# A segment-recurrent attention and MLP kernel: left outputs in a PSUM bank of their own, and one left K pass in another kind of segment

## The chip, the cores and the metric

One core of one Trainium2 chip. The metric is the device time of one execution in microseconds; the time before is the median of three runs.

## The reference

The input x (2048 tokens of 1024 columns) is normalised, and three things are added: x itself, an MLP with gelu (1024 to 3584 to 1024), and a recurrent attention with 32 heads of 128 columns. The recurrence is what matters here (biases and the batch of 1 left out):

```python
for s in range(64):                                  # segments of 32 tokens
    h = concat([mem, xn[32 * s:32 * s + 32]])        # 8 memory rows + 32 tokens
    q, k, v = h @ Wq, h @ Wk, h @ Wv                 # 1024 -> 32 heads x 128
    p = softmax(mask(q @ k.T * scale))               # memory rows see all, tokens are causal
    o = (p @ v) @ Wo                                 # 4096 -> 1024
    mem = o[:8]                                      # the next segment needs it
    outs.append(o[8:])
```

Everything is bfloat16 in and out. The 64 segments depend on each other through the 8 memory rows.

## The kernel before

A first part (normalisation and MLP) runs up to about 430 us; it leaves x plus MLP output in a DRAM buffer `R_n`, which `turn_R` lays out again into `res_d` (per segment) and `resL_d` (per group). Then comes the loop over the 64 segments, written out by hand, and nearly all of the change lies there.

**Rows.** [...] A segment has 40 rows. So 32 of them are "main" rows (24 tokens and 8 memory rows, tile `hT`) and the last 8 tokens of a segment are "left" rows. The left rows of four segments make one group of 32 rows (`hL`), which goes through the weights once for four segments. Left rows need no memory of their own segment to be projected, so their passes can be made early or late. `hL` has four slots, one for each segment of the group, renewed one after the other for the next group (`load_left_rows` by DMA into a raw place, `renew_left` by VectorE or GpSimd into `hL`).

**Units and kinds.** The weights of a segment are 64 units of 128 x 2048: K, Q and V in halves u = 0 and 1 with eight units each (`half_pass`), then 16 units of O (`o_product`). One unit against one set of rows is four 512-column matmuls on the four column groups of TensorE. 47 units live in SBUF; 17 are "streamed" into six buffers again in every segment, by DMAs on SyncE's queue (`start_stream`, issued when a streamed unit is done), two of them copied by VectorE out of PSUM banks in which they are kept (L283). The kind of a segment is `i4 = s % 4`. The tables `PLACED`, `SCORES_0`, `SUMS_0`, `VALUES_0`, `SUMS_1`, `VALUES_1` say for each kind in which order the units come and behind which unit the scores, the sums of the softmax and the values are put into TensorE's order. Left passes are made in kind 0 (K0 and K1), kind 1 (V0), kind 2 (Q0 and V1) and kind 3 (Q1, and O for the whole group).

**The order in a segment.** K0, Q0, K1 (in it `scores(0)`), Q1 (in it `sums(0)`), V0, V1 (in it `scores(1)`, `values(0)`, `sums(1)`), O (in it `values(1)`), and the turn. `exps`, `weights` and the transposes between them are on ScalarE and VectorE, in order. `weights(0)` writes its second part, `pdB` (L1032), into slot i4 of `ko[0]` in kinds 0, 1 and 3. `ko[u]` holds, slot by slot, first the left keys, then these weights, then the left rows of the attention's output, which kind 3's O product reads. `ko[0]` is the second half of `d_oL`.

**The turn.** The memory rows of O's result become part of the next segment's `hT`: `put_mem` multiplies by an identity into `mixed` (L343), VectorE copies them (L353). While this goes on TensorE is filled with left products of the next segment: `lead_products` makes up to six units of the pass named in L1235 from resident weights, four of them ahead of `put_mem` and two behind. In kinds 0 to 2 O's main result is made in two halves of a PSUM bank and added up (`fold`, L1233). In kind 3 one bank holds left and main rows side by side, eight 512-column matmuls for a unit, and ScalarE copies it out (L1229).

**Outputs.** VectorE adds the residual (L1252), and the rows go out by DMAs: in kinds 0 to 2 four on `loads` (ScalarE's queue in the first seven segments, then GpSimd's), in kind 3 two on ScalarE's queue and six on GpSimd's.

**PSUM.** Three banks rotate (`new_acc`, `let_go`), one is `mixed`, four keep streamed units. 

Of the kernel before, what the change touches and what calls it, by code (L numbers as in the profile page):

```python
# [14 lines left out]
ALU = mybir.AluOpType  # L15
# [53 lines left out]
LATE_FROM = 5  # L69
BEGUN = 4  # L70
# [56 lines left out]
def kernel(  # L127
# [244 lines left out]
    with tc.tile_pool(name="ma", bufs=2) as ma:  # L372
# [138 lines left out]
        def with_left(seg):  # L511

            return seg % GRP == GRP - 1

        def turn_R(ttg, eng, small=None):

            for i in range(4):
                seg = 4 * ttg + i  # L520
                rows = R_n[seg * SEG:(seg + 1) * SEG, :].rearrange("t (j c) -> t j c", j=4)
                og, slot = divmod(seg, GRP)
                both = [
                    t.rearrange("(h r) c -> r h c", h=2)
                    for t in (res_d[GRP * og + GRP, :, :], resL_d[og, :, :])
                ]
                halves = [rows.rearrange("t (h w) c -> t w h c", w=2)[:, w, :, :] for w in range(2)]
                if with_left(seg):
                    m0 = SEG
                    pairs = [(both[w][m0:m0 + SEG, :, :], halves[w]) for w in range(2)]  # L530
                else:
                    pairs = [(res_d[seg + 1, :, :].rearrange("(j t) c -> t j c", j=4), rows)]
                pairs += [(both[w][slot:SEG:GRP, :, :], halves[w][NX:SEG, :, :]) for w in range(2)]
# [220 lines left out]
    with tc.tile_pool(name="late", bufs=1) as late:  # L754
# [67 lines left out]
        raw_2, raw_3, raw_01 = VL[1][:, 0:64], VL[0][:, 256:320], VL[0][:, 256:384]  # L822
        led = {}

        for s in range(NSEG):
# [12 lines left out]
            left_k = [i4 == 0] * 2  # L838
# [94 lines left out]
            def turn_kL(ps, u):  # L933
                turn(ps, ko[u], nc.vector.tensor_copy if first else nc.scalar.copy)
# [24 lines left out]
            def scores(u):  # L959
# [12 lines left out]
                for j in range(4):  # L972
                    q = slice(32 * j, 32 * j + 32)
                    nc.tensor.matmul(  # L974
                        sB[q, :, :, :], lhsT=keys[:, j, :, i4], rhs=qL_ends[:, 4 * j:4 * j + 4, :, :],
# [63 lines left out]
            def values(u, rs):  # L1039

                V, (pdA, pdB) = st["V", u], st["pd", u]
                av = {r: new_acc() for r in rs}
# [15 lines left out]
                for r in rs:  # L1058
# [8 lines left out]
                    let_go(av[r])  # L1067
# [10 lines left out]
            def o_product(n, t, acc):  # L1078
# [4 lines left out]
                for k in range(2):  # L1083
                    h = 4 * (i % 4) + 2 * u + k
                    main = (outM if i >= 4 else nat_home)[:, h, :]
                    if left_o:
                        lhs = [(0, 32, ko[i // 4][:, h, :]), (32, 32, main)]
                        tiles = [(64 * r + r0, w, (2 * r, 2 * r + 1), lhsT) for r0, w, lhsT in lhs for r in range(2)]
                        start, stop = n == 0 and k == 0, n == 15 and k == 1
                    elif n < NPAIR:  # L1090
                        tiles = [(64 * k + 32 * r, 32, (2 * k + r, 2 - 2 * k + r), main) for r in range(2)]
                        start, stop = n == 0, n == NPAIR - 1
                    else:
                        tiles = [(32 * r, 32, (r,), main) for r in range(4)]
                        start, stop = n == NPAIR and k == 0, n == 15 and k == 1
                    for r0, rows, blocks, lhsT in tiles:
                        nc.tensor.matmul(  # L1097
                            acc[r0:r0 + rows, 0:256 * len(blocks)],
                            lhsT=lhsT,
# [30 lines left out]
            turn_k(psK, 0)  # L1130
            if first:
# [15 lines left out]
            if i4 == 0 and not first and more:  # L1147
                renew_left(raw_01, 0, 2, mover)
# [13 lines left out]
            if i4 == 3 and more:  # L1162
                renew_left(raw_3, 3, 4, mover)
# [37 lines left out]
            if i4 == 1 and more:  # L1201
                load_left_rows(g + 1, 2, 3, raw_2)
            if i4 == 2 and more:
                load_left_rows(g + 1, 3, 4, raw_3)
            if i4 == 3 and g + 2 < NGRP:
                load_left_rows(g + 2, 0, 2, raw_01)
# [107 lines left out]
```

## Time and profile before

| | |
|---|---|
| median of 3 runs | 1741.6 us (1738.84 to 1742.26) |
| the profiled execution | 1743.2 us |
| its span, first to last instruction | 1741.5 us |
| granted TensorE clock | 1.0 |
| moved by DMA | 579.36 MB, 333 GB/s over the span |

In the profile PE is TensorE's matmuls and PEld its weight loads, DVE is VectorE, ACT is ScalarE, POOL is GpSimd and SP is SyncE. Rows in order of time give start, duration, engine, line, operation, operands and the count of merged instructions; a bracket gives the idle time ahead and what seems to have ended it. Matmuls overlap in the array: the time that one costs is read from the distance of the starts, not from its duration. Rows of groups give the busy time, the mean of one in ns and the idle time ahead of them. Rows of stretches give the busy time of each engine, the granted clock, the share of the DMA engines and GB/s.

### The profile page before, as it was taken

The page shows a single profiled execution, that of the slowest core. Times are in us where ns is not written, and L with a number is a line of the kernel's source. Part 1 is how long each engine was busy: PE and PEld are TensorE (multiplying, and loading weights), DVE is VectorE, ACT ScalarE, POOL GpSimd, SP SyncE. Part 2 cuts the span into 40 slices and gives each one's busy share as a digit, 9 for nine tenths or more (in the row PEclk, how much of TensorE's full clock was granted, in tenths as well). Part 3 has the DMA queues.
Part 4 walks back from the last instruction along what each step waited for, and adds up shares of the span by engine and source line. Part 5 has one row for each costly group of instructions (what it writes and reads, how often), then busy time and mean ns, then how long its engine had stood idle before and what let it go on. Part 6 is the DMA issues. An engine that isn't in the chain of part 4 may idle for free. (4 is left out here: it accounts for less than half of the span.)

```text
span 1741.5 us, 66351 instructions
## 1 busy us (share of the span) xinstructions
PE 1685.8 (97%) x28367; PEld 837.6 (48%) x28367; DVE 1040.8 (60%) x2657; ACT 702.1 (40%) x1742; POOL 287.2 (16%) x575
## 2 busy tenths in 40 slices
PE   9999999999999999999999999999999999999998
PEld 5444444444444454444444445444544444454544
DVE  7658383835656565656556565656565656565565
ACT  6335160712333443444344444444434444443333
POOL 0000001412210211121112111121212121111121
PEclk9999999999999999999999999999999999999999
DMA  9446311879999999999999999999999999999997
GB/s 278 156 149 190 89 51 41 273 257 353 377 385 365 378 398 378 392 388 384 377 389 384 387 390 385 394 370 400 383 398 384 396 377 390 381 395 373 390 378 308
DMA packets 236635, 579.36 MB, mean 333 GB/s; under 512 B 63747, under 2 KB 92611, under 8 KB 236340
## 3 DMA queue, kind: packets, MB, share of 16 engines
q1 hardware_dynamic: 204222, 555.52, 84.9%
q0 software_dynamic: 15680, 14.35, 2.5%
q10 hardware_dynamic: 16438, 5.25, 1.2%
q8 instruction: 222, 3.64, 0.8%
q14 instruction: 73, 0.60, 0.1%
HBM read 558.98 MB, written 26.54 MB: 336 GB/s over the span
## 5 line engine op out<-in xcount | busy, mean ns | idle before, releaser
L855 PE MATMUL acc<-u,hr_home 128*32 128x512 bf16 x11456 | 760.1, 380 | 16.4 <-DMA u<-Wc_V 7.4
L855 PEld LDWEIGHTS <-hr_home 128*32 128x32 bf16 x12288 | 336.3, 97 | 314.1 <-issue 41.1
L855 PE MATMUL acc<-u,hrL 128*32 128x512 bf16 x2991 | 257.8, 380 | 0.0
L549 PE MATMUL ps<-u 128*128 128x512 bf16 (+1 forms) x992 | 195.3, 359 | 1.0 <-DMA u<-in_B_w_dram 0.9
L909 ACT CAST d_oL<-acc 128x512 bf16<-128x512 f32 x143 | 83.0, 583 | 247.2 <-PE acc L855 207.1
L283 DVE TENSOR_SCALAR u<-kept 128x512 uint32<-128x512 uint32 x254 | 162.1, 679 | 31.7 <-PE acc L855 23.0
L1097 PE MATMUL acc<-u,d_oL 128*32 128x512 bf16 x2560 | 161.8, 380 | 5.7 <-DMA u<-Wc_O 5.3
L1097 PE MATMUL acc<-u,kq 128*32 128x256 bf16 (+1 forms) x2688 | 137.0, 319 | 14.4 <-DMA u<-Wc_O 12.8
L680 PE MATMUL ps<-u 128*128 128x512 bf16 x672 | 146.0, 380 | 0.0
L549 PEld LDWEIGHTS <-u 128*128 128x128 bf16 x992 | 91.5, 98 | 103.5 <-DMA u<-in_B_w_dram 1.7
L1097 PEld LDWEIGHTS <-kq 128*32 128x32 bf16 x3328 | 87.2, 96 | 92.0 <-issue 24.3
L1028 DVE TENSOR_TENSOR pd_main<-kq,mixed 128x320 bf16<-128x320 bf16 x128 | 62.5, 488 | 110.0 <-ACT mixed L1015 110.0
L1276 POOL DMA_DIRECT2D out_dram<-hr_home x168 | 85.0, 513 | 254.4 <-DVE hr_home L1252 254.0
L939 ACT CAST kq<-acc 128x256 bf16<-128x256 f32 x256 | 89.0, 375 | 90.7 <-PE acc L855 52.7
L992 DVE TENSOR_TENSOR kq<-kq,mixed 128x96 bf16<-128x96 bf16 x128 | 26.2, 205 | 161.6 <-ACT kq L985 84.6
L855 PEld LDWEIGHTS <-hrL 128*32 128x32 bf16 x3200 | 85.8, 97 | 49.8 <-issue 4.2
L943 DVE STREAM_TRANSPOSE kq<-kq 128x256 bf16<-128x256 bf16 x256 | 98.1, 421 | 16.3 <-ACT kq L939 16.2
L913 ACT CAST kq<-acc 128x512 bf16<-128x512 f32 x128 | 75.1, 587 | 79.4 <-PE mixed L974 78.0
L680 PEld LDWEIGHTS <-u 128*128 128x128 bf16 x672 | 65.4, 98 | 78.9 <-DVE u L637 0.4
L629 ACT ACTIVATE u<-ps,b1col 128x512 bf16<-128x512 f32 x112 | 76.4, 683 | 65.3 <-PE ps L549 63.3
L1015 ACT ACTIVATE mixed<-mixed,small_consts 128x160 f32<-128x160 f32 x256 | 94.2, 368 | 8.4
L1097 PEld LDWEIGHTS <-d_oL 128*32 128x32 bf16 x2560 | 65.5, 96 | 61.0 <-issue 6.5
(142 smaller groups left out, 1912.3 us busy)
## 6 DMA issues: line engine op xcount, KB each, us to landing
u<-Wc_K SPq DMA_DIRECT2D x256, 512.0 KB
u<-Wc_O SPq DMA_DIRECT2D x256, 512.0 KB
u<-Wc_Q SPq DMA_DIRECT2D x192, 512.0 KB
u<-Wc_V SPq DMA_DIRECT2D x192, 512.0 KB
u<-Wc_V SPq DMA_DIRECT2D x63, 320.0 KB
u<-in_B_w_dram SPq DMA_DIRECT2D x28, 512.0 KB
u<-in_A_Wq_dram SPq DMA_DIRECT2D x13, 512.0 KB
u<-in_A_Wv_dram SPq DMA_DIRECT2D x12, 512.0 KB
```

The source lines that it names most:

```text
L283: nc.vector.tensor_single_scalar(out=out, in_=in_, scalar=0, op=ALU.bitwise_or)
L549: nc.tensor.matmul(ps[:, SEG * s0:SEG * s1].rearrange("p (s t) -> p s t", t=SEG), lhsT=w1_sb[fb // 2][:, kt, (fb % 2) * P:(fb % 2 + 1) * P ...
L629: nc.scalar.activation(out=xb[:, :], in_=ps[:, :], func=ACT.Identity, bias=b1col[:, fb:fb + 1], scale=1.0)
L680: nc.tensor.matmul(ps[:, :], lhsT=gts[fc // 4][:, fc % 4, t * P:(t + 1) * P], rhs=w2_sb[fc // 2][:, fc % 2, cs], start=(fc == 0), stop=(fc ...
L855: nc.tensor.matmul(o, lhsT=lhs[:, i, :], rhs=m, start=(i == seq[0]), stop=(i == seq[-1]), tile_position=(0, 32 * j),)
L909: cp(out=out, in_=ps.rearrange("p (h e) -> p h e", e=32))
L913: cp(out=t[:, :], in_=ps[:, :])
L939: nc.scalar.copy(out=q_home[:, h0:h1, NL:40], in_=ps[:, 32 * h0:32 * h1].rearrange("p (h e) -> p h e", e=32))
L943: nc.vector.transpose(out=half, in_=half)
L1015: nc.scalar.activation(out=mixed[:, 160 * b:160 * b + 160], in_=mixed[:, 0:160], func=ACT.Exp, scale=-1.0, bias=off[:, b:b + 1],)
L1097: nc.tensor.matmul(acc[r0:r0 + rows, 0:256 * len(blocks)], lhsT=lhsT, skip_group_check=True, rhs=o_columns(t, k, blocks), start=start, sto ...
L1276: loads.dma_start(out=out_flat[rows, 256 * j:256 * j + 256], in_=res[32 * j:32 * j + NX, :])
```

## The change

- Kind 3 makes main outputs as the other kinds do (`fold`, then L1233's addition). Left outputs go into a PSUM bank of their own, `st["psL"]`, by a new `left_product`: eight 256-column matmuls for a unit. A streamed unit's left product is made behind its main product; those of resident units are queued in `later` and made at the rate of `LEFT_RATE`, the last six (`LEFT_BEHIND`) in the turn, four ahead of `put_mem` and two behind, where the filler of kind 3's turn was K0 of the next kind 0. To save a bank, `values(1)` of kind 3 puts one of its results in `mixed`.
- `left_out` adds the left residual into the first half of `ko[0]` and sends it by four DMAs on GpSimd, behind the four main output DMAs.
- The left K0 pass is made in kind 1 (for slots 1 to 3 of the group, and slot 0 of the next), K1's stays in kind 0. Kind 0's turn leads K0 instead of V0, which is made wholly in kind 1's pass. The keys of slot 0 wait in `keys_0` and `keys_1`, in places of `VL`.
- The left rows are renewed at other times: slot 0 behind K1 of kind 0, slot 1 behind K0 of kind 1, slot 3 in kind 3's turn, ahead of the output DMAs on GpSimd. Their loads move by an O pass or behind `values(1)`.
- `turn_R` issues 8 DMAs for four segments instead of 13.

The core of the diff (the renaming of raw places and the shorter `turn_R` are cut):

```diff
+LEFT_BEHIND = 6
+LEFT_RATE = (0, 0, 0, 0, 0, 1, 1, 2, 1, 0, 0, 0, 0, 0, 0, 0)
...
-            left_k = [i4 == 0] * 2
+            left_k = [first or i4 == 1, i4 == 0]
...
+            def left_product(n, t, acc):
+
+                w, i, u = O_UNITS[n]
+                for k in range(2):
+                    lhs = ko[i // 4][:, 4 * (i % 4) + 2 * u + k, :]
+                    for r in range(4):
+                        nc.tensor.matmul(
+                            acc[32 * r:32 * r + 32, 0:256], lhsT=lhs, rhs=o_columns(t, k, (r,)), skip_group_check=True,
+                            start=st["left"] == 0, stop=st["left"] == 31, tile_position=(0, 32 * r),
+                        )
+                    st["left"] += 1
...
             def turn_kL(ps, u):
-                turn(ps, ko[u], nc.vector.tensor_copy if first else nc.scalar.copy)
+                if first or u:
+                    turn(ps, ko[u], nc.vector.tensor_copy if first else nc.scalar.copy)
+                    return
+                flat = q_all[:, 0:512]
+                turn(ps, flat.rearrange("p (h t) -> p h t", h=16), nc.scalar.copy)
+                slots = flat.rearrange("p (n s) -> p n s", s=GRP)
+                if s > 1:
+                    nc.vector.tensor_copy(out=ko_slots[0][:, :, 1:GRP], in_=slots[:, :, 1:GRP])
+                nc.vector.tensor_copy(out=keys_0, in_=slots[:, :, 0])
...
-                av = {r: new_acc() for r in rs}
+                av = {r: mixed if u and r and left_o else new_acc() for r in rs}
...
+            if i4 == 1 and s > 1 and more:
+                renew_left(raw_01[:, 64:128], 1, 2, mover)
...
             for n, unit in enumerate(O_UNITS):
                 t = unit_tile(unit)
-                if n == NPAIR and not left_o:
+                if n == NPAIR:
                     st["folded"] = fold(psX)
                     psX = new_acc()
                 o_product(n, t, psX)
+                if left_o:
+                    if IS_STREAMED[unit]:
+                        left_product(n, t, st["psL"])
+                    else:
+                        later.append(n)
+                    for _ in range(LEFT_RATE[n]):
+                        if later:
+                            make_left(later.popleft())
                 unit_done(unit)
...
+            while left_o and len(later) > rest:
+                make_left(later.popleft())
+
+            def left_out():
+
+                nc.vector.tensor_tensor(out=ko_flat[0][:, 0:256], in0=st["psL"][:, 0:256], in1=st["resL"], op=ALU.add)
+                let_go(st["psL"])
+                left_to = out_flat[g * GRP * SEG:(g + 1) * GRP * SEG, :].rearrange("(s t) c -> t s c", s=GRP)[NX:SEG]
+                for j in range(4):
+                    eng = (nc.sync if j % 2 else nc.scalar) if final else nc.gpsimd
+                    eng.dma_start(
+                        out=left_to[:, :, 256 * j:256 * j + 256], in_=ko_flat[0][32 * j:32 * j + 32, 0:256],
+                    )
...
+            if left_o and not final:
+                for _ in range(LEAD_FIRST):
+                    if later:
+                        make_left(later.popleft())
+                put_mem(o_sb, nxt["hT"], mixed[:, 224:288])
+                while later:
+                    make_left(later.popleft())
+            elif not final:
+                w, u = (("K", 0), ("Q", 0), ("Q", 1))[i4]
...
+            nc.vector.tensor_tensor(out=r_rows, in0=o_sb[:, 0:8, :], in1=r_rows, op=ALU.add)
             let_go(psX)
+            if i4 == 3 and more:
+                renew_left(raw_3, 3, 4, mover)
+            for j in range(4):
+                eng = (nc.scalar if j % 2 else nc.sync) if final else loads
+                eng.dma_start(out=out_flat[rows, 256 * j:256 * j + 256], in_=res[32 * j:32 * j + NX, :])
+            if left_o:
+                left_out()
```

More of the change, by code (lines that the diff above doesn't have):

```diff
@@ L520, in turn_R @@
                 seg = 4 * ttg + i
+                og, slot = divmod(seg, GRP)
                 rows = R_n[seg * SEG:(seg + 1) * SEG, :].rearrange("t (j c) -> t j c", j=4)
[L522 to L525, printed above, removed]
-                ]
[L527 to L533, printed above, removed]
+                pairs = [
+                    (res_d[seg + 1, :, :].rearrange("(j t) c -> t j c", j=4), rows),
+                    (
+                        resL_d[og, :, :].rearrange("(j t s) c -> t j s c", j=4, s=GRP)[:, :, slot, :],
+                        rows[NX:SEG, :, :],
+                    ),
+                ]
                 for o, r in pairs:
@@ L973, in scores @@
                     q = slice(32 * j, 32 * j + 32)
+                    own = keys_1[:, 32 * j:32 * j + 32] if u == i4 == 0 and not first else keys[:, j, :, i4]
                     nc.tensor.matmul(
-                        sB[q, :, :, :], lhsT=keys[:, j, :, i4], rhs=qL_ends[:, 4 * j:4 * j + 4, :, :],
+                        sB[q, :, :, :], lhsT=own, rhs=qL_ends[:, 4 * j:4 * j + 4, :, :],
                         start=False, stop=True, skip_group_check=True, tile_position=(0, 32 * j),
@@ L1066, in values @@
                         cp(out=out.rearrange("p (b c) q -> p c b q", b=2), in_=oV[r][:, :, :, q0:q1])
-                    let_go(av[r])
+                    if av[r] is not mixed:
+                        let_go(av[r])
             def o_columns(t, k, blocks):
@@ L1267 @@
[L1267 to L1276 removed]
+            r_rows = res.rearrange("p (h e) -> p h e", e=32)
```

105 lines of the change are left out of this document (33 added, 72 removed).

## The prediction

> **What bounds the kernel now.** I read the page first, then the stretches of the recurrence by kind (kind = segment number mod 4; a segment runs from one memory matmul at L343 to the next), then the order of time of PE, DVE and POOL around the places that the change touches.
>
> ```profile
> PE 1685.8 (97%) x28367; PEld 837.6 (48%) x28367; DVE 1040.8 (60%) x2657; ACT 702.1 (40%) x1742; POOL 287.2 (16%) x575
> core 0: us, PE busy (x) PEld busy (x) DVE busy (x) ACT busy (x) POOL busy (x), PEclk, DMA share, GB/s
> 664.80:1654.90 990.10, 959.06 (x19708) 486.49 (x19705) 590.58 (x1524) 409.06 (x1116) 184.35 (x360) 1.00 1.01 386
> 1323.80:1344.10 20.30, 19.87 (x421) 9.96 (x418) 12.52 (x33) 8.90 (x24) 4.73 (x9) 1.00 0.99 367
> 1016.90:1035.60 18.70, 18.37 (x386) 9.31 (x382) 11.61 (x31) 7.83 (x22) 3.15 (x6) 1.00 1.03 402
> 1363.90:1384.10 20.20, 20.17 (x418) 10.37 (x414) 13.09 (x33) 8.88 (x24) 3.49 (x7) 1.00 1.02 396
> 1056.50:1077.70 21.20, 20.98 (x430) 10.75 (x430) 11.54 (x30) 8.54 (x23) 4.03 (x8) 1.00 1.02 397
> ```
>
> PE is busy 97% of the span, at full clock. The long stretch holds twelve groups of four segments: 990.1 / 12 = 82.5 us each. The four rows below it are the quietest segments of kinds 0, 1, 2 and 3: 20.3 + 18.7 + 20.2 + 21.2 = 80.4 us is what PE's own order takes when nothing comes late. So 2.1 us a group are waits. The weights that stream in are close behind: 386 GB/s x 82.5 us = 31.8 MB a group, and at the 402 GB/s of the busiest row that alone takes 79.2 us. PE and the transfers are nearly equal, and kind 1, short by 1.5 us and more, is where the transfers cannot follow; in kind 0, slow at 367 GB/s, they find no free slots.
>
> ```profile
> L855 PE MATMUL acc<-u,hr_home 128*32 128x512 bf16 x8592 | 568.1, 380 | 11.2 <-DVE u L283 4.0 <-DMA u<-Wc_V 2.8 <-DMA u<-Wc_Q 2.6
> L1097 PE MATMUL acc<-u,kq 128*32 128x512 bf16 x864 | 59.4, 381 | 6.3 <-DMA u<-Wc_O 6.0 <-ACT kq L1066 0.2
> ```
>
> These groups (of that long stretch) show who is late: stream tiles by DMA, and tiles that DVE copies out of PSUM (L283).
>
> **The change: PE's work moves and does not shrink.** Rows of a turn of kind 3, then of kind 0, then the end of kind 0's O loop:
>
> ```profile
> 1076.76 0.82 PE L855 MATMUL acc<-low,hrL 128*32 128x512 bf16 x12
> 1078.36 0.39 PE L855 MATMUL acc<-u,hr_home 128*32 128x512 bf16 x4
> ...
> 1260.43 1.06 PE L1097 MATMUL acc<-u,kq 128*32 128x256 bf16 x32
> 1261.31 1.04 PE L855 MATMUL acc<-u,hrL 128*32 128x512 bf16 x16
> 1262.52 0.21 PE L343 MATMUL mixed<-ident_mem,kq 128*128 128x32 bf16 x2 [0.17 <-DVE kq L1233]
> 1262.67 0.61 PE L855 MATMUL acc<-u,hrL 128*32 128x512 bf16 x8
> 1263.11 0.39 PE L855 MATMUL acc<-low,hr_home 128*32 128x512 bf16 x4
> ```
>
> Eight 512-wide matmuls take 1263.11 - 1262.67 = 0.44 us, a unit's four 0.22. Thirty-two 256-wide ones take 1261.31 - 1260.43 = 0.88, a unit's eight 0.22 as well. Kind 3's O loop is now 16 units of 8 wide matmuls; it becomes 12 x 4 wide and 4 x 8 narrow for the main rows plus 16 x 8 narrow for the left rows: 128 matmuls become 208, and the time stays 32 x 0.22 = 7.0 us. Zero is my value for the 80 more; where that loop end holds one late tile it reads about 1.0 us for 32, so the bound above is 0.12 x 5 = 0.6 us a group (160 narrow ones). The turn gains nothing: kind 3's takes 1078.36 - 1076.76 = 1.60 us with six units of filler, kind 0's 1263.11 - 1261.31 = 1.80 with six. The ACT copy that goes (L1229) and the two output DMAs that leave ACT's queue lie beside PE work, hence zero.
>
> Moves: K0's left pass leaves kind 0 (its two units after the turn, -0.44) and kind 3's turn, and comes to kind 0's turn and kind 1; V0's six filler units go back into kind 1's pass, so that kind 1 has eight more units in all (two of K0, six of V0, +1.8); kind 3 no longer holds the four K0 filler units ahead of its memory matmul, and two of its left units slip behind it (six units, -1.3). The quiet lengths become 19.9, 20.5, 20.2 and 19.9: the same 80.4 but for rounding, and even. That is the good side: kind 1 no longer outruns 19.8 us of transfers (79.2 / 4). I let it recover kind 1's 0.8 and kind 0's 0.4 of the 2.1, **1.2 us a group**; the other 0.9 are L283 copies and jitter that stay.
>
> **New wait 1, kind 3's values.** In kind 0 and in kind 3:
>
> ```profile
> 1338.01 0.24 PE L1001 MATMUL mixed<-kq,small_consts 128*32 128x160 bf16 x4
> 1340.07 0.32 PE L1047 MATMUL acc<-pd_main,kq 64*128 64x80 bf16 x8 [0.25 <-DVE pd_main L1028]
> 1340.39 0.23 PE L1053 MATMUL acc<-kq,VL 64*128 64x128 bf16 x2
> ...
> 1069.08 0.25 PE L1001 MATMUL mixed<-kq,small_consts 128*32 128x160 bf16 x4
> 1069.44 2.33 PE L1097 MATMUL acc<-u,d_oL 128*32 128x512 bf16 x40
> 1071.70 0.32 PE L1047 MATMUL acc<-pd_main,kq 64*128 64x80 bf16 x8
> ```
>
> From sums to values the softmax chain needs 2.06 us (kind 0, which waits there). Kind 3 has 2.62 now, because five O units fill ten rounds. Afterwards they fill six (five main, one left): 0.36 + 6 x 0.22 = 1.67, so PE waits 0.4, and 0.1 more for L1053's operand: **+0.5** (0 to 0.6).
>
> **New wait 2, kind 1's first scores.** DVE and PE there:
>
> ```profile
> 1100.32 1.29 DVE L283 TENSOR_SCALAR u<-kept 128x512 uint32<-128x512 uint32 x2 [0.85 <-DMA u<-Wc_K]
> 1101.85 0.71 DVE L927 STREAM_TRANSPOSE d_oL<-d_oL 128x512 bf16<-128x512 bf16 x1 [0.24 <-ACT d_oL L909]
> 1102.49 0.18 DVE L951 COPY kq<-qL 128x128 bf16<-128x128 bf16 x1
> 1103.32 0.77 DVE L943 STREAM_TRANSPOSE kq<-kq 128x256 bf16<-128x256 bf16 x2 [0.45 <-ACT kq L939]
> 1104.20 0.27 PE L968 MATMUL mixed<-kq,d_oL 128*32 128x40 bf16 x16
> ```
>
> DVE ends at 1104.09, PE starts the scores at 1104.20: 0.1 of slack. The left keys add behind L283 a transpose (0.7), a copy of 384 columns (0.2 to 0.5, from L951's 128) and one of 128 (0.2): 1.1 to 1.4, of which DVE's two pauses (0.24 + 0.45) and the slack take 0.8. PE and L283 both move back 0.44. **+0.4** (0 to 0.6).
>
> **New wait 3, kind 0's first weights, the largest.** The left outputs now leave from the first half of ko[0], in four POOL DMAs behind the four main ones; kind 0's weights (L1032) write into those columns and must wait until all four have landed. DVE is in order, so the second queries' transposes and through them the second scores stand behind it.
>
> ```profile
> 1323.78 0.26 PE L343 MATMUL mixed<-ident_mem,kq 128*128 128x16 bf16 x4
> 1334.66 0.44 DVE L1032 TENSOR_TENSOR d_oL<-kq,mixed 128x128 bf16<-128x128 bf16 x1
> 1335.28 0.77 DVE L943 STREAM_TRANSPOSE kq<-kq 128x256 bf16<-128x256 bf16 x2
> 1335.77 0.60 PE L968 MATMUL mixed<-kq,d_oL 128*32 128x40 bf16 x16
> ...
> 1325.04 1.03 POOL L1264 DMA_DIRECT2D out_dram<-pd_main  x2 [6.00 <-DVE hr_home L1252]
> 1326.20 1.17 POOL L1258 DMA_DIRECT2D out_dram<-hr_home  x2
> 1327.37 0.55 POOL L1264 DMA_DIRECT2D out_dram<-hr_home  x1
> 1329.08 0.55 POOL L1264 DMA_DIRECT2D out_dram<-hr_home  x1 [1.16 <-PE acc L855]
> ...
> 1079.18 1.03 POOL L1264 DMA_DIRECT2D out_dram<-pd_main  x2 [6.20 <-DVE hr_home L1252]
> 1084.34 0.55 POOL L1264 DMA_DIRECT2D out_dram<-hr_home  x1 [2.29 <-DMA u<-Wc_V]
> ...
> 1098.65 0.22 PE L343 MATMUL mixed<-ident_mem,kq 128*128 128x32 bf16 x2
> 1099.88 2.02 POOL L1276 DMA_DIRECT2D out_dram<-hr_home  x4 [6.39 <-DVE hr_home L1252]
> ...
> DMA to landing us min/median/max: 3.8/4.6/5.5
> ```
>
> L1032 starts 1334.66 - 1323.78 = 10.9 us behind the memory matmul; without K0's two left units 10.4. The scores behind it have no slack: their 16 matmuls already stretch to 0.60 us where wait 2's take 0.27. The POOL rows: five output DMAs issue without a pause, the sixth comes 4.0 and 5.2 us behind the first (1329.08 - 1325.04, 1084.34 - 1079.18), about when the first lands; the releasers named are not the cause. Afterwards there are eight: main ones at 1.23 to 3.25 (rows of 1099.88 against 1098.65), the sixth at 5.3 to 6.4, the eighth two issues of 0.59 (1326.20) later at 6.5 to 7.6. The 16 KB DMAs of L1258 land in 4.6 us (last row): at 11.1 to 12.2, a wait of 0.7 to 1.8. I take **+1.5**, above the middle, since the moved copy of left rows (renew_left of slot 3) stands ahead of all eight on POOL and can only delay them. Bounds: 6.5 + 3.8 = 10.3, no wait; or the eighth waits until the first left one has landed, 3.25 + 4.6 = 7.9, + 5.5 = 13.4, a wait of 3.0.
>
> [...]
>
> Smaller edits: the preparation of R issues 8 DMAs instead of 13 for four segments, the same bytes, on SP and POOL, away from PE's path: 0, at most 2 us of gain in the first segments. Segment 1 gets a K0 left pass of its own, 8 x 0.22 = 1.7 us once, where loads bind anyway. 0 for both together.
>
> **Sum.** Wait 3 falls into 14 groups (in the first the main outputs go by ACT's queue, the last has no successor): 14 x 1.5 = 21. Waits 1 and 2: 15 x 0.9 = 13.5. Recovered: 15 x 1.2 = 18. Net +16.5 us on the profiled execution's 1743.2 (span 1741.5 and 1.7 around it), which lies 1.6 above the median of the runs; 1741.6 + 16.5 = **1758 us**.
>
> **Rivals.** (1) Faster: the left outputs land ahead of 10.4 us, and the evened-out kinds let transfers keep up. Point of decision: the eighth issue at 5.8 or earlier. Then there is no wait 3 and 1741.6 + 13.5 - 18 = 1737; if waits 1 and 2 are at their lower ends as well, 1741.6 - 18 = 1724. For it: all kinds at 20 us against 19.8 of transfers; against it: the pause ahead of the sixth DMA. 0.22. (2) No change that shows: wait 3 is a scrape of 0.3 us, 14 x 0.3 = 4, and 1737 + 4 = 1741. 0.10. (3) Slower still: the eighth waits for the first left one, 14 x 3.0 = 42 in place of 21: 1779; 0.08. (4) Narrow matmuls cost their 0.6: +9, 1767, inside the range. My forecast, with (4), has 0.60.
>
> About 0.2% (3.5 us) is what a measurement of this kernel can tell from no change. Below 1738: 0.22; within: 0.10; above 1745: 0.68. The range goes from 1732, inside rival 1, to 1776, wait 3 at 2.8 us; the likeliest case alone spans 1747 to 1772.
>
> **What would show it.** Right: in kind 0 DVE stands ahead of its first weights until an output DMA of the left rows lands, and kind 0 grows to 21 us and more; PE waits 0.3 to 0.6 ahead of kind 1's first scores and of kind 3's values; kind 1's tile waits go. Wrong: the first weights start 10.4 us behind the memory matmul; or POOL issues eight outputs without a pause; or narrow matmuls further apart than 28 ns in kind 3.

## The result, and the profile after

The changed kernel takes 1812.4 us (median of four executions, 1800.4 to 1817.0) against 1741.3 before: 1.040 times as long, interval 1.0345 to 1.0454. The forecast was 1758 in a range of 1732 to 1776: the right side, with the wait that it named as the largest part, but outside the range, and with a growth that is four times too small. The profiled execution has a span of 1815.3 us. The page's first part, the mean granted clock, and then three stretches: a segment of kind 0 with a long wait, one with a short wait, and twelve groups of four segments.

```profile
PE 1707.2 (94%) x29649; PEld 879.5 (48%) x29649; DVE 1067.4 (59%) x2740; ACT 701.4 (39%) x1744; POOL 288.8 (16%) x587
```

```profile
core 0: 1815.3 us, clock 0.984
```

```profile
1023.50:1050.50 27.00, 21.13 (x419) 10.48 (x416) 12.21 (x32) 8.32 (x23) 5.85 (x11) 0.87 0.79 271
938.20:960.10 21.90, 19.57 (x419) 10.47 (x416) 12.04 (x32) 8.32 (x23) 6.19 (x12) 1.00 0.98 363
651.30:1702.80 1051.50, 977.25 (x20640) 517.60 (x20640) 609.68 (x1584) 407.52 (x1116) 205.85 (x408) 0.98 0.97 363
```

PE is busy for 21 us more and idle for 52 us more. Twelve groups take 1051.5 us, 87.6 each, where they took 82.5. The third column from the right is the granted clock: 1.00 in the stretches before, here 0.98, and 0.87 in the segment with the long wait. The four executions had a mean clock of 0.984, 0.984, 0.987 and 0.992, the shortest one the highest. Who waits, over the whole span (PE, then DVE):

```profile
PE mixed L981 <- DVE kq L956: 48.3, 16, 5.6
PE acc L872 <- issue: 8.6, 7, 1.7
PE acc L1108 <- DMA u<-Wc_O: 6.3, 14, 1.3
...
DVE d_oL L1046 <- DMA out_dram<-d_oL: 47.8, 15, 5.6
```

Fifteen times DVE stands at the left part of kind 0's first weights (L1046, L1032 before) until the left outputs have landed, 3.2 us each and up to 5.6; behind it stand the transposes of L956, and behind them PE's second scores (L981). The order of time in the turn at 1023.5, POOL and then DVE and PE:

```profile
1024.56 0.52 POOL L1299 DMA_DIRECT2D out_dram<-hr_home  x1 [2.02 <-DVE hr_home L1293]
1025.31 1.51 POOL L1299 DMA_DIRECT2D out_dram<-hr_home  x3 [0.23 <-issue]
1026.89 0.60 POOL L1267 DMA_DIRECT2D out_dram<-d_oL  x1
1028.90 0.58 POOL L1267 DMA_DIRECT2D out_dram<-d_oL  x1 [1.41 <-issue]
1030.30 0.55 POOL L1267 DMA_DIRECT2D out_dram<-d_oL  x1 [0.81 <-issue]
1033.07 0.55 POOL L1267 DMA_DIRECT2D out_dram<-d_oL  x1 [2.22 <-PE acc L848]
...
1039.53 0.43 DVE L1046 TENSOR_TENSOR d_oL<-kq,mixed 128x128 bf16<-128x128 bf16 x1 [5.58 <-DMA out_dram<-d_oL]
...
1040.64 0.65 PE L981 MATMUL mixed<-kq,d_oL 128*32 128x40 bf16 x16 [5.59 <-DVE kq L956]
```

Five output transfers go out at once, as before. The sixth comes 4.3 us behind the first (1028.90 - 1024.56), but the seventh and eighth pause again, and the eighth is issued 9.6 us behind the segment's start. DVE goes on 6.5 us after that (1039.53 - 1033.07). This is the turn with the longest wait. In the 14 turns with eight outputs on POOL the eighth is issued 7.6 to 9.8 us behind the start (median 8.7), and the last one lands at 12.1 to 15.9.

The trace also has the time of each landing, and it tells what the pauses wait for. The sixth is issued 0.3 us behind the landing of the first, in all 14 turns. The seventh is issued 0.3 us behind the landing of the third in 10 turns, and right behind the sixth in the other four. The eighth is issued 0.3 us behind the landing of the fifth, which is the first left one, in 12 turns, and right behind the seventh in the other two.

Around the end of the wait the clock is halved:

```profile
1038.40:1045.20 6.80, 4.46 (x70) 1.93 (x73) 2.40 (x8) 2.34 (x8) 0.00 (x0) 0.50 0.41 154
```

Mean length of a segment from the fourth on, in us (from one memory matmul to the next, as in the prediction), with PE's idle time in it by what ended it, over 60 ns (eng: another engine; DMA; issue: nothing that the profile names). These are worked out from each trace's records; the runs of the last rows are told below.

```
                     kind 0  kind 1  kind 2  kind 3   group | idle a group: eng  DMA  issue
before                20.76   19.69   20.58   21.66   82.69 |               0.82 1.66  0.13
after                 24.41   20.38   20.74   21.90   87.44 |               4.26 0.44  1.14
e2  own place         20.85   20.17   20.76   21.70   83.49 |               1.46 0.67  0.93
e5  before, split     20.73   19.76   20.43   24.54   85.46 |               0.66 1.71  2.28
e6  e2 + wide left    21.00   20.12   20.59   20.78   82.49 |               1.48 0.74  0.00
e8  after + filler    23.31   20.26   20.93   21.91   86.41 |               1.67 0.67  1.16
e12 after, left first 21.93   20.34   20.89   21.97   85.12 |               2.80 0.55  1.00
e13 best              20.80   20.23   20.36   20.92   82.31 |               1.32 0.62  0.10
```

Kind 0 takes 3.65 of the 4.75 us that a group grows by. The DMA column falls from 1.66 to 0.44, the recovery that the prediction counted on. The last column is new and was not forecast.

### The profile page after: what moved, and what is told of

The parts are those of the page before. It is cut to its first block, busy times and chain, and to the rows that moved or that the text cites. A ratio compares the mean times of both kernels' runs of the same rounds, so it can differ in the third digit from the quotient of the medians.

```text
span 1815.3 us, 69019 instructions
## 1 busy us (share of the span) xinstructions
PE 1707.2 (94%) x29649; PEld 879.5 (48%) x29649; DVE 1067.4 (59%) x2740; ACT 701.4 (39%) x1744; POOL 288.8 (16%) x587
## 5 line engine op out<-in xcount | busy, mean ns | idle before, releaser
L848 PE MATMUL acc<-u,hr_home 128*32 128x512 bf16 x11456 | 789.3, 385 | 9.9 <-DVE u L285 5.0
L848 PE MATMUL acc<-u,hrL 128*32 128x512 bf16 x3011 | 272.5, 380 | 0.0
L914 ACT CAST d_oL<-acc 128x512 bf16<-128x512 f32 x128 | 74.6, 583 | 219.9 <-PE acc L848 189.8
L1299 POOL DMA_DIRECT2D out_dram<-hr_home x224 | 114.0, 516 | 249.8 <-DVE hr_home L1293 248.0
L1108 PE MATMUL acc<-u,d_oL 128*32 128x512 bf16 x2048 | 147.7, 388 | 5.1 <-DMA u<-Wc_O 2.8
L1108 PE MATMUL acc<-u,kq 128*32 128x256 bf16 (+1 forms) x2560 | 117.8, 295 | 7.9 <-issue 3.7
L848 PEld LDWEIGHTS <-hrL 128*32 128x32 bf16 x3232 | 90.2, 97 | 56.6 <-issue 4.3
L1108 PEld LDWEIGHTS <-kq 128*32 128x32 bf16 x3072 | 81.0, 96 | 58.4 <-ACT kq L1080 21.4
L956 DVE STREAM_TRANSPOSE kq<-kq 128x256 bf16<-128x256 bf16 x256 | 97.9, 421 | 13.4 <-ACT kq L952 13.3
L981 PE MATMUL mixed<-kq,d_oL 128*32 128x40 bf16 x2048 | 46.0, 182 | 54.3 <-DVE kq L956 48.3
```

The costliest lines, as they stand in the source:

```text
L848: nc.tensor.matmul(o, lhsT=lhs[:, i, :], rhs=m, start=(i == seq[0]), stop=(i == seq[-1]), tile_position=(0, 32 * j),)
L914: cp(out=out, in_=ps.rearrange("p (h e) -> p h e", e=32))
L956: nc.vector.transpose(out=half, in_=half)
L1108: nc.tensor.matmul(acc[r0:r0 + 32, 0:256 * len(blocks)], lhsT=main, skip_group_check=True, rhs=o_columns(t, k, blocks), start=start, stop= ...
L1299: eng.dma_start(out=out_flat[rows, 256 * j:256 * j + 256], in_=res[32 * j:32 * j + NX, :])
```

## The experiments

Theory: the landing of the left outputs holds kind 0, the idle time halves the clock behind it, and PE's sequencer runs out of instructions in kind 3. Rival: the moved K pass and the narrow matmuls cost the time, and the wait is only where the slack shows. Line numbers in the rows below are the changed kernel's or, where an edit added lines, up to nine higher; those of e5 follow the kernel before, with its narrow matmuls at L1090.

**e1: the left outputs on ScalarE's queue.**

```
-                    eng = (nc.sync if j % 2 else nc.scalar) if final else nc.gpsimd
+                    eng = (nc.sync if j % 2 else nc.scalar) if final else nc.scalar
```

> The changed kernel with one edit: the four transfers of the left outputs go out from ScalarE's queue and no longer from POOL's, where they are the 5th to 8th output transfers of the turn. Theory (the left outputs' late landing holds kind 0's weights, and the idle TensorE that follows halves its clock): DVE's wait at the weights' second product for these transfers falls from 47.8 us to under 5, TensorE's idle time ahead of the second scores from 51 us to under 8, the half-clock windows behind it go (mean granted clock from 0.984 to 0.995 or more), and of the +71 us the 48 of the wait and the 25 of the clock go: 1735 to 1755 us, what is left over 1741 being the stalls of TensorE's own sequencer (16 us) less what was recovered in waits on weights. Rival (the moved K pass and the 256 wide matmuls cost the time and the wait is only where the slack shows): the idle time turns up ahead of other lines and the time stays at 1790 us or more.

Measured: 1769.3 us, 1.0171 [1.0141, 1.0202]. The wait for the landing is gone from DVE's list, and so are the half-clock windows behind it, but for one at 506 us, in the first of these segments. That is the theory's side, 14 us above its range. In e2 below, where the transfers stay on POOL, the time is 12 us lower, so most of the 14 is the price of ScalarE's queue:

```profile
1009.75 2.82 ACTq L1267 DMA_DIRECT2D out_dram<-d_oL  x4
1012.66 0.59 ACT L914 CAST d_oL<-acc 128x512 bf16<-128x512 f32 x1 [7.44 <-DMA out_dram<-d_oL]
```

ScalarE spends 2.82 us on issuing four transfers, and its evacuation of kind 0's first keys stands behind them. The landing in the bracket is hardly what it waited for: the cast starts 0.1 us behind the end of the fourth issue (1009.75 + 2.82 = 1012.57).

**e2: another place for the weights, transfers still on POOL.**

```
-                place = qL_slots[0] if first or VALUES_0[i4][0] < VALUES_0[i4][1] else ko_slots[0]
+                place = qL_slots[0] if first or i4 == 0 or VALUES_0[i4][0] < VALUES_0[i4][1] else ko_slots[0]
```

> The changed kernel with one edit: kind 0's weights write their left part into the first buffer of the left queries, as the other kinds may, and not into the buffer from which the left outputs are sent; the transfers stay on POOL. Theory: DVE no longer waits for the landing; the next writer of that buffer is the evacuation of kind 0's values on ScalarE, some 13.5 us behind the turn, when the transfers (landing 12.1 to 15.9 us behind it) are nearly through. A wait of 0 to 2 us a group stays there, partly hidden, no half-clock windows: 1740 to 1770 us. Rival (moved K pass and narrow matmuls): 1790 us or more.

Measured: 1757.5 us, 1.0096 [1.0062, 1.0130]. DVE no longer waits for the left outputs, and the clock is at 1.000. The next writer of their buffer, ScalarE's evacuation of kind 0's values (L1080), still waits for them in 6 of 15 turns, 4.5 us in all, as the expectation allowed, and PE waits behind it (over the twelve groups):

```profile
PE acc L1108 <- ACT d_oL L1080: 3.6, 5, 1.5
```

So 54.9 of the 71 us hung on that one place of the weights, and a few more hang on the buffer still. Kind 0 goes from 24.41 to 20.85, with 2.51 us of this being idle time (3.59 to 1.08). The other 1.05 us is time in which PE was busy. I put it down to the clock, 15 x 1.05 = 16 us, which e8 tests. This is the version with the smallest edit, and it is still 16 us above the kernel before.

**e8: more work for PE, the wait left in.** (e4 was a first form of it, in which the filler stood behind the first unit of the second values pass.)

```
+            if i4 == 0 and not first:
+                spare = banks.tile([P, 512], F32, name="acc", tag=free_banks[0])
+                w = next(res_tiles[unit] for unit in O_UNITS if not IS_STREAMED[unit] and unit not in LATE)
+                for _ in range(11):
+                    nc.tensor.matmul(spare[0:32, :], lhsT=w[:, 0:32], rhs=w[:, 0:512], start=True, stop=True, ...)
             psV1, psV1L = half_pass("V", 1, left_v[1], at)
```

> The changed kernel with the wait left in, but TensorE kept busy in it: ahead of kind 0's second scores stand 14 more matmuls of 512 columns (about 14 x 0.22 = 3.0 us) on weights that lie in SBUF, into a spare bank that nobody reads. They leave the transfers and DVE's wait as they are. Theory (the long idle time halves the clock for 3.4 or 6.8 us behind it, which costs about 25 us): no window of half clock behind this place, mean granted clock 0.995 or more, DVE's wait for the transfers still 45 to 52 us, and 1785 to 1800 us. Rival (the clock costs nothing that the wait doesn't cost already, the windows lie over other waits): 1810 to 1835 us, the dummies adding what exceeds the stall in the turns where it is short.

> The changed kernel with the wait left in and TensorE kept busy ahead of it: 11 matmuls of 512 columns (11 x 0.22 = 2.4 us) on weights that lie in SBUF, into the bank that the second half of the values' pass takes next, stand ahead of kind 0's second values pass, so they start without a wait and the idle time at the second scores shrinks from 3.5 to about 1.3 us a group. Nobody reads what they write. Theory (an idle time of over 2.5 us halves the clock in the following 3.4 or 6.8 us): the lost clock falls from 27 us to under 6, the wait on the transfers stays, the time is the changed kernel's less about 16 us of clock plus about 7 where the stall was shorter than the filler: 1800 to 1808 us. Rival (the clock costs nothing beside the wait): 1815 to 1825 us.

e4 measured 1839.5 us, 1.0588 [1.0542, 1.0634], and says little of the clock: the filler itself waited for its bank,

```profile
PE acc L1193 <- ACT kq L953: 37.2, 15, 4.5
```

so its 3 us were added and not put into the gap. In e8 the filler takes the bank that is free at that time. It measured 1799.8 us, 1.0343 [1.0317, 1.0369]: 2.4 us of useless work in each group, and by the medians the kernel is 12.7 us faster. The interval overlaps a little with the changed kernel's (1.0345 to 1.0454), so the size is read from the traces. Waits of DVE and PE, and the stretch of twelve groups:

```profile
DVE d_oL L1047 <- DMA out_dram<-d_oL: 39.0, 15, 5.2
...
PE mixed L982 <- DVE kq L957: 7.6, 8, 2.6
```

```profile
651.30:1702.80 1051.50, 1008.69 (x21157) 540.23 (x21150) 620.00 (x1616) 415.43 (x1139) 208.54 (x415) 1.00 0.99 370
```

DVE's wait is still there (39.0 of 47.8), PE's idle time at the second scores is filled, and the clock is at 1.00. The filler and the idle time that it fills cancel out in kind 0 (2.4 against 3.59 - 1.17), so what is gained is clock: 1.10 us a segment of kind 0, 15 x 1.10 = 16 us in these traces, the same as e2 gave.

**e12: the left outputs first in POOL's queue.** `left_out()` is called ahead of the loop over the main outputs and not behind it.

> The changed kernel with one edit: the left outputs are added and sent ahead of the main outputs of the turn, so they are POOL's 1st to 4th output transfers and the main ones the 5th to 8th. Same transfers, same queue, same buffers. Theory (the left outputs land late because POOL's 6th to 8th transfer each waits for an earlier one to land before it can be issued): the left outputs land before 9 us behind the turn, DVE's wait for them falls from 47.8 us to under 8 us, the half-clock windows go, 1752 to 1768 us. Rival (they land late because they are slow in themselves, rows of 512 bytes scattered over the output): the wait stays above 25 us and the time at 1785 us or more.

Measured: 1774.6 us, 1.0203 [1.0169, 1.0237], between the two. DVE's wait is 17.5 us in the twelve groups in which it had been 41.9: less, but not gone. POOL in one of the turns:

```profile
928.73 1.72 POOL L1267 DMA_DIRECT2D out_dram<-d_oL  x3 [2.18 <-DVE d_oL L1262]
934.57 0.55 POOL L1267 DMA_DIRECT2D out_dram<-d_oL  x1 [4.12 <-issue]
935.11 2.07 POOL L1301 DMA_DIRECT2D out_dram<-hr_home  x4
```

Now the fourth transfer pauses, 5.8 us behind the first, and then the four main ones go out in a row. In all 14 turns with eight outputs the fourth is issued 0.3 us behind the landing of the first. The left transfers are not slow in themselves, as the rival had it: from issue to landing left ones take 5.2 us and main ones 4.5 in the median in this turn, and both 5.0 over the changed kernel. Ahead of the first pause POOL issued three of the left ones here, and four main ones and one left one in the changed kernel. What limits it is not shown. It is not the number of transfers, by which the prediction read its rows ("the sixth"). It is not their bytes either: the first five of the kernel before, 68 KB, go out together, and four left ones, 64 KB, do not.

**e5: the kernel before, kind 3's O product in narrow matmuls.** The same columns, 256 matmuls for 128.

```
-  tiles = [(64 * r + r0, w, (2 * r, 2 * r + 1), lhsT) for r0, w, lhsT in lhs for r in range(2)]   # 512 wide
+  the same tiles, each as two matmuls: acc[r0:r0 + rows, 256 * half:256 * half + 256], half = 0, 1
```

> The kernel before with one edit: each 512 wide matmul of kind 3's O product is made as two of 256, so the same columns with 128 matmuls and 128 weight loads more in each group of four kinds, as narrow as the changed kernel's. Theory (TensorE's sequencer stalls at every 256th instruction where the instructions are used up faster than they are fetched): one or two stalls of 0.5 to 1.75 us more per group, 1750 to 1766 us, and gaps that nothing releases ahead of kind 3's O product, each at the same remainder of the instruction number by 256. Rival (narrow matmuls cost nothing, as the prediction had it: 32 in 0.88 us): 1739 to 1745 us.

Measured: 1787.2 us, 1.0283 [1.0249, 1.0318], the theory's side and 21 us above its range. Narrow matmuls alone cost 46 us in a kernel in which nothing else was changed. Two groups of them in the twelve groups' stretch (count, then busy us, mean ns, then idle us and what ended it), and PE in one turn:

```profile
L1090 PE MATMUL acc<-u,d_oL 128*32 128x256 bf16 x1664 | 53.6, 274 | 13.3 <-issue 12.7 <-DMA u<-Wc_O 0.4
L1090 PE MATMUL acc<-u,kq 128*32 128x256 bf16 x1248 | 44.9, 277 | 11.6 <-issue 11.4
```

```profile
1095.40 1.06 PE L1090 MATMUL acc<-u,kq 128*32 128x256 bf16 x32
1096.27 0.38 PE L1090 MATMUL acc<-W_O,kq 128*32 128x256 bf16 x3
1098.40 0.95 PE L1090 MATMUL acc<-W_O,kq 128*32 128x256 bf16 x27 [1.75 <-issue]
```

In the middle of a unit, on a resident weight, PE stops for 1.75 us and the profile names no releaser. I numbered PE's instructions in order of time: matmuls, weight loads and its sequencer's few semaphore instructions. Divided by 256, the number of the first instruction behind the gap leaves 193 in all 27 such gaps of e5's recurrence, in e2 in 18 of 19, and in the changed kernel in all 16 of over 0.3 us from 430 us on. The instruction queue moves about one packet for every 256 of them:

```profile
q8 instruction: 232, 3.80, 0.8%
```

3.80 MB in 232 packets (the changed kernel's) is 16.4 KB each (16384 bytes in the trace). Its PE instructions are 59555, which is 232.6 times 256; in the kernel before 222 packets go with 56973, 222.6 times 256. By an estimate from these counts a packet is a block of 256 of PE's instructions, 64 bytes each (16384 / 256). The trace's times of these packets go with the gaps: for each gap of over 0.5 us from 450 us on, 22 in e5, 11 in e2 and 15 in the changed kernel, one of them had ended 1.2 to 1.6 us ahead of the gap's end. That PE waited for the block is my reading of these times.

The gaps also go with the time in which PE uses up such a block: in the kernel before the shortest is 4.99 us and the stalls come to 1.9 us. In e2 all 14 blocks used up in 4.5 to 4.7 us stall, by 0.3 to 1.6 us each, and of those that last 5.4 us or more few do. In e5 the blocks of 3.7 to 4.6 us stall by up to 2.3. Blocks with their stalls mostly last 5 to 6.2 us. The packet itself takes 1.0 us in the median; what the rest of the time goes to is not shown. The stalls come to 35 of the 46 us. Of the rest, the three windows of half clock in e5's groups can hold 5 (3 x 3.41 / 2); what remains is not accounted for.

**e6: wide left products, on top of e2.**

```
-                    for r in range(4):
-                        nc.tensor.matmul(acc[32 * r:32 * r + 32, 0:256], lhsT=lhs, rhs=o_columns(t, k, (r,)), ...)
+                    for r in range(2):
+                        r0 = 64 * k + 32 * r
+                        nc.tensor.matmul(acc[r0:r0 + 32, :], lhsT=lhs, rhs=o_columns(t, k, (2 * k + r, 2 - 2 * k + r)), ...)
...
+  left_out: ScalarE copies one half of the partitions, DVE the other and makes two additions
```

> The kernel with the weights in their own place, and the left products made of 64 matmuls of 512 columns a group instead of 128 of 256, into two halves of a bank that are added behind the turn (a ScalarE copy, a DVE copy and one add more before the left outputs). Theory (what is left of the +16 us is TensorE's sequencer waiting for instructions: 14.3 us in 19 gaps, each at the 194th of 256 instructions, behind blocks that are used up in 4.4 to 4.7 us): no block of 256 instructions is used up in under 5 us any more, the sequencer's stalls fall below 4 us in all, and the time goes to 1742 to 1749 us. Rival (the moved K pass and the shape of the work cost it, and the stalls only stand where TensorE would have waited anyway): 1753 to 1760 us with the stalls gone and other waits in their place.

Measured: 1743.5 us, 1.0022 [1.0008, 1.0035], as the theory had it. No block is used up in under 5.63 us, and no stall of the sequencer is left; kind 3 falls from 21.70 to 20.78, shorter than before the change. PE's waits over the twelve groups, with no issue row among them:

```profile
PE acc L848 <- DVE u L285: 7.5, 19, 0.5
PE acc L1109 <- DMA u<-Wc_O: 3.7, 6, 1.2
PE acc L1062 <- DVE pd_main L1043: 3.2, 13, 0.3
```

The first row is the price: DVE adds the halves before it restores the weights kept in PSUM. In e2 it was 5.1 us, 10 times. The tail behind the last memory matmul is longer too, 29.5 us where the kernel before has 26.1 and e2 26.7. On the other side the wait behind L1080 is gone as well. So the step from e2 is a balance, estimated from these rows: 14 us of stalls and 15 x 0.3 = 4 us of that wait are gained, 15 x 0.2 = 3 us for the halves and 3 us in the tail are lost, which makes 12 of the measured 14.0.

**e7: nothing behind the turn, on top of e2.** `LEFT_BEHIND = 6` becomes 0.

> The kernel with the weights in their own place, and no unit of the left outputs made behind the turn of kind 3: all stand ahead of it. Theory: TensorE gets 48 matmuls of 27 ns (1.3 us a group) ahead of the turn and has nothing to do while DVE adds the output and turns it, so the turn of kind 3 idles by 0.9 to 1.5 us a group more: 1757 plus 13 to 21, that is 1770 to 1778 us, with TensorE's idle time ahead of the first products of memory and behind them up by as much. Rival (units behind the turn cost as much as they hide, since the left outputs and their transfers go out later for them): 1750 to 1762 us.

Measured: 1764.9 us, 1.0133 [1.0109, 1.0157], 7.4 above e2, between the theory's range and the rival's: the six units behind the turn are worth about half of what I expected. Kind 3 grows by 0.42 us, where 1.3 us of work moved ahead of the turn.

**Towards a better version: e9, e10, e11, e13.** e9 gives kind 3's main outputs the first free bank; e10 lets ScalarE make both copies and has no halves in the last turn; e11 has five units behind the turn; e13 is e10 with the sum ahead of the main outputs' issue.

> The kernel with the weights in their own place and wide left products, and one edit more: kind 3's main outputs take the bank that comes free first and the left outputs the next one. Theory (the main product of kind 3 starts 0.2 to 0.4 us late for its bank): kind 3 is 0.2 to 0.4 us shorter, 3 to 6 us in all: 1738 to 1745 us. Rival (the start of the main product is hidden by the units in flight): the same as without the edit within 2 us.

> The kernel with the weights in their own place and wide left products, with a shorter sum of their two halves: ScalarE makes both copies, so DVE has two additions instead of a copy and two additions behind the turn (0.44 us less before it restores the weights that are kept in PSUM), and in the last turn, where nothing follows, the products are narrow and no halves are added. Theory (what the wide products cost is the sum on DVE, for which TensorE waits 0.3 to 0.5 us a group at the first weights that DVE restores, and 3.5 us in the tail): 15 x 0.4 = 6 us and 1.5 to 3 us in the tail less than 1743.5: 1734 to 1738 us. Rival (those waits move to another place of the turn): 1741 to 1745 us.

> The same with five units of the left outputs behind the turn instead of six, so the last left product ends 0.22 us earlier and the main outputs' turn starts 0.22 us later. Theory (six is about what the turn hides): within 3 us of the kernel with six. Rival (the sum of the halves is what is waited for at the start of kind 0): 2 to 4 us faster.

> The kernel with its own place, wide left products and the short sum, and one edit more: the halves of the left outputs are added before the main outputs' transfers are issued, not behind them. In the later groups POOL issues those transfers and nothing changes. In the first group of the recurrence ScalarE issues them (1.9 us), its copies of the halves stand behind that, DVE's restored weights behind the copies, and TensorE waited 3.5 us there (its segment took 26.4 us where the others of its kind take 20.4 to 21.0). Theory: that wait falls below 1 us and the time by 3 to 5 us, to 1736 to 1740 us, just below the kernel before. Rival (the first group waits for its weights anyway): 1741 to 1744 us.

e9: 1749.4 us, 1.0049 [1.0033, 1.0064], above e6, though the intervals touch; the bank's order does not pay. e10: 1742.0, 1.0015 [0.9998, 1.0031]; its rival was right. In this turn PE waits about as long as e6's row has it (7.5 / 19 = 0.4 us):

```profile
918.42 0.36 ACT L1269 COPY d_oL<-acc 64x256 f32<-64x256 f32 x1
...
918.82 0.42 DVE L1270 TENSOR_TENSOR pd_main<-acc,pd_main 128x256 bf16<-128x256 f32 x1 [0.96 <-PE acc L848]
...
919.28 0.42 DVE L1271 TENSOR_TENSOR d_oL<-d_oL,pd_main 128x256 bf16<-128x256 f32 x1
919.62 1.28 DVE L285 TENSOR_SCALAR u<-kept 128x512 uint32<-128x512 uint32 x2
...
920.96 1.26 PE L848 MATMUL acc<-u,hr_home 128*32 128x512 bf16 x20 [0.42 <-DVE u L285]
```

DVE's first addition starts only when ScalarE's second copy is through (918.42 + 0.36 = 918.78), and so in all 15 turns, 0.03 us behind it; the copy that DVE was spared became a wait. e11: 1743.0, 1.0019 [1.0003, 1.0035]; kind 0 gains 0.25 us and kind 3 loses 0.28. e13: 1739.7, 1.0001 [0.9987, 1.0015]. The segment behind the first group went from 26.4 to 22.5 us as expected, but the interval holds no change against the kernel before, so no version was found that beats it.

## What of the prediction held, and where it failed

**Wait 3, the step that failed.** The place of the wait, its rows and its victims are those forecast. The step that failed is the one from the sixth transfer to the eighth. The sixth waits for the landing of the first, as the prediction read it from the rows of before. It then let the seventh and the eighth follow at 0.59 us each, and no turn of the kernel before has a seventh output that could have shown it. In the runs these wait for landings too: the eighth goes out when the first left one has landed, 7.6 to 9.8 us behind the segment's start and not at 6.5 to 7.6. That is rival 3 as it was written, with the landing at 13.4 and a wait of 3.0; measured are 12.1 to 15.9 and a wait of 3.2 on the mean. It had been given a chance of 0.08. What the edit of e2 takes away is 55 us, where the term had 21.

**The term that was missing: the clock.** 38 of those 55 us are idle time (15 x 2.51) and 16 are the half clock behind it. The prediction read a granted clock of 1.00 and let PE's speed stand while it gave PE idle times of up to 3 us. The longest idle time of PE in the recurrence of before is 1.7 us, so no row there could price it; but that a wait has an aftermath was not weighed at all.

**Narrow matmuls: zero, and rival (4) at 9 us, both too low.** The 27 ns between them was right (busy rows show no loss), but the price lies in the instructions. In e2 the sequencer stalls are 0.93 us a group, 14 us in all, against the 0.6 of the rival's bound. The bound had been read from how far the matmuls start apart, and the stalls are not in that. The waits of the kernel before, over the twelve groups, held a hint that the prediction passed over, an idle time that nothing released:

```profile
PE acc L1097 <- issue: 1.1, 2, 0.7
```

With rival 3's 1779, 16 us for the clock and 14 for the stalls the sum would have been 1809 us against 1812. That it comes so near is in part luck, since other terms were off too.

**Waits 1 and 2**, read in one turn each. Kind 1's first scores stretch to 0.48 us from 0.27 (first row), so wait 2 is 0.2 and not 0.4. For kind 3's values (the other rows):

```profile
1056.44 0.48 PE L981 MATMUL mixed<-kq,d_oL 128*32 128x40 bf16 x16
...
1629.10 0.41 PE L848 MATMUL acc<-u,hr_home 128*32 128x512 bf16 x4
1629.55 1.27 PE L1108 MATMUL acc<-u,d_oL 128*32 128x512 bf16 x16
...
1630.85 0.40 PE L1108 MATMUL acc<-u,d_oL 128*32 128x512 bf16 x4
1631.18 0.21 PE L1061 MATMUL acc<-pd_main,kq 64*128 64x80 bf16 x1
1631.38 0.19 PE L1061 MATMUL mixed<-pd_main,kq 64*128 64x80 bf16 x1
```

With four wide matmuls in 0.22 us, the O loop begins 0.23 us late (1629.55 - 1629.32), the values 0.11 us late (1631.18 - 1631.07), and their second half 0.20 behind the first: 0.5 together, the forecast's size, though half of it in places that it did not name.

**What was recovered.** Forecast: 1.2 us a group, 18 in all. Idle time ended by DMA went from 1.66 to 0.44 us a group, 15 x 1.22 = 18. In e2, where the long waits are gone, 1.0 is kept, 15 us. So the good side of the change is real and about of the size forecast.

**The quiet lengths** were forecast as 19.9, 20.5, 20.2 and 19.9. In e2 the shortest segments are 19.83, 20.03, 20.21 and 20.83: kinds 0 to 2 within 0.5, kind 3 0.9 longer (0.6 in e6, where the stalls are gone).

From the changed kernel to e13 the steps are 54.9 us (place), 14.0 (wide), 3.8 (the sum of the halves, near the noise). With the first two the changed design stands where the kernel before stood: it wins 15 to 18 us of waits on weights, and pays, by an estimate from the rows above, about as much for waits 1 and 2 (15 x 0.7 = 10) and for adding the halves (3, and 3 in the tail). How much the moved K pass alone costs or brings was not tried.

## What to carry to other kernels

Here the write into a buffer from which an output leaves waited until the transfer had landed, 3.2 us on the mean and up to 5.6; a step that reuses such a buffer must be priced against the last transfer of the queue, with every pause ahead of it, not the first pause only. A wait on the critical engine is not priced by its length alone: in the changed kernel's recurrence all nine idle times of TensorE over 2.8 us came with a window of 3.41 or 6.83 us at half clock, and two of the seven from 1.6 to 2.8 us did. Filler put into the wait can then be worth more than it costs: in e8 2.4 us of it a group made the kernel 12.7 us faster. Splitting matmuls at the same columns was not free either, 46 us in e5: count the instructions of the densest stretch, and ask how long 256 of them last. Under 5 us was mostly too short here: in the changed kernel 12 of 15 such blocks were followed by a stall, of 0.23 to 1.75 us.

## What the runs showed of the hardware

**The clock.** In the changed kernel's recurrence every idle time of PE over 2.8 us (nine of them, 3.24 to 5.59 us) came with the granted clock of 0.50, for windows of 3.41 or 6.83 us that began from 2.2 us ahead of its end to 1.4 us behind it. Of the seven from 1.6 to 2.8 us two did and five did not: one of 1.69 us did, one of 2.72 us did not. One of 2.50 us did as well (at 598.3 us, the window of 3.41 us beginning at 601.5).

**The instruction supply.** In the changed kernel, from 430 us on, all 16 idle times of PE over 0.3 us (0.35 to 1.75 us) for which the profile names no releaser end at an instruction whose number leaves 193 when divided by 256, and 1.2 to 1.6 us behind the end of a packet of 16384 bytes on the instruction queue. In e2 and e5 a block of 256 that was used up in under 5 us was followed by a stall of 0.3 to 2.3 us in most cases.

**Queues for outputs.** In the changed kernel POOL paused at the sixth of eight outputs in all 14 turns, at the seventh and the eighth in most (1.41, 0.81 and 2.22 us in the turn at 1023.5), and in e12, where the 16 KB left ones came ahead of the 12 KB main ones, at the fourth (4.12 us in the turn shown). The sixth, and in e12 the fourth, was issued 0.3 us behind the landing of the first. ScalarE spent 2.82 us of its own time to issue four.
